# Fused attention, soft mixture of experts and feed-forward: the drain of attention reordered, w1 read by contiguous rows, three more places for weights, w_in narrowed in the experts, passage reordered

## The chip, the cores and the metric

The kernel runs on one core of one Trainium2 chip. The metric is the device time of one execution in microseconds (us), as the median over runs. Five engines work side by side and wait for each other by semaphores: TensorE (PE; its weight loads are shown apart as PEld), VectorE (DVE), ScalarE (ACT), GpSimd (POOL) and SyncE (SP). SP issues nearly all DMA transfers here, in one queue, in program order.

## The reference

```python
# attention: q, k, v are (4, 8, 576, 64); factor = 4
out_d     = sm_attn(mean4(q), mean4(k), mean4(v))      # on means of 4 tokens
out_up    = np.repeat(out_d, 4, axis=2)
out_local = softmax(where(|i - j| < 4, q k^T / 8, -1e9)) @ v
x = (out_up + out_local) as (2304, 512)
# soft mixture: phi (512, 32), w1 (8, 512, 1024), w2 (8, 1024, 512)
logits     = x @ phi
slot_input = softmax(logits, over tokens).T @ x        # 32 slots, 4 an expert
slot_out_e = relu(slot_input_e @ w1[e]) @ w2[e]
x = softmax(logits, over slots) @ slot_out
# feed-forward: w_in (512, 2048), w_out (2048, 512), both float64
h = relu(x @ w_in);  out = h * h @ w_out
```

## The kernel before, in words

**Attention** (to about 153 us) takes 16 units of two heads, in a software pipeline whose steps are single letters with a lag each; a table gives the order of the letters for each of 19 rounds. Each unit's output `xt` gives its share of the logits (`lgt`), and is transposed into token rows (`xk`, and `xr` for the last 64 tokens). Batch by batch, the softmax over tokens runs on with a running maximum `mb` and a factor `al` that rescales what has been summed: `acc = acc * al + new` (line 695) is the input of the 32 slots before normalisation, in four groups of rows.

**The drain** (lines 797 to 833) finishes the last batch. The exponentials `ee` are transposed and copied (`et`, `etr`); `mb` is transposed and its maximum over the four groups is taken (`mrow`); from it come the weights `wt` and the sum `ws`, and by `scales` the selection matrix `selw`, which joins the four groups and normalises. Four matmuls (`stp`) with the weights `acc` and the moving `selw` give `sT`, the transposed slot inputs. `busy(n)` issues n padding matmuls whose result nobody reads; `CHAIN` says how many stand at three places of the drain, and `FN` how many in each attention round.

**The experts** (lines 878 to 961): for each of eight, `expert_up` multiplies `sT` with the four pieces of w1 (`hp`, 32 matmuls), ScalarE applies relu (`hs`), a transpose (`htp`, copied to `ht`) and `expert_down` with four pieces of w2 (`so`, 32 matmuls) follow. Beside them run the softmax over slots (`gate_soft`, `gate_rows`) and, after two w2 pieces of expert 6, copies of the gates (`crp` into `cst`). `NEXP` says after which w2 piece of which expert a step of narrowing is recorded.

**Narrowing**: w_in and w_out come as float64 (pairs of 32-bit words) and become float32 by five operations on each 128 x 512 piece; the first, an absolute value, is on VectorE up to the end of the experts and on ScalarE after (`act_abs`). `NORDER` is the order of the pieces; `narrow_turn` goes one operation further with the pieces in hand, and begins the next turn's pieces ahead. `split_wout` (ScalarE) and `split_low` (VectorE) then split a w_out piece in a high part and a rest.

**The passage** (table `ACHAIN`): `S` copies `so` to `sos`, `T` transposes it to `soT` (`sotp`), `a` multiplies it with w_in (`ap`, copied to `asb`), `r` spreads it into rows (`arp`, copied to `ast`), `g` copies gates, `n` steps the narrowing, `W` splits a w_out piece, `f` issues padding matmuls, and `u` makes the first products `up` of the final stage.

**The final stage** (lines 1135 to 1160) runs 96 steps, 6 chunks of 384 tokens by 16 pieces of 128 hidden columns: one matmul `up`, relu (`r`), squares, high part `ghi` and rest `glo`, and nine matmuls `po`.

**Loads.** The weights are cut into loads of 128 x 4096 bytes. The list `loads` is w1 and w2 expert by expert, w_in 0 put in after the 43rd load (`LPOS`), then `TAIL`. `load_next` issues from the list's head as long as a place is free: 32 places of a ring, a few of other pools, among them two opened late in attention (`NLA`) and six opened when the tiles of the last unit are done (`NLB`). A place is free again when its piece's last matmul or narrowing is recorded, and the transfer then waits in the queue for that instruction. Each load also waits for the eighth load before it to land.

Of the kernel before, what the change touches and what calls it, by code (L numbers as in the profile page):

```python
# [20 lines left out]
NU = B * NP  # L21
DM = 512
# [27 lines left out]
FN = {'F': [0, 1, 1, 0, 0, 0, 0, 0, 0, 0, 0, 0, 0, 0, 0, 4, 0, 10, 0, 0], 'H': [10, 5, 2, 0, 0, 0, 0, 0, 0, 0, 0, 0, 0, 0, 0, 1, 0, 4, 6, 0], 'J': [1, 4, 3, 0, 0, 0, 0, 0, 0, 0, 0, 0, 0, 0, 0, 0, 7, 3, 0, 0]}  # L50
# [6 lines left out]
CHAIN = (5, 4, 4)  # L57
# [3 lines left out]

LPOS = [43, 43, 43, 43]
TAIL = 'o0 o1 i1 o2 o3 o4 o5 o6 o7 i2 o8 o9 o10 o11 i3 o12 o13 o14 o15'
SLOTS = {16: ['i1'], 20: ['r1'], 40: ['i2'], 44: ['r2'], 60: ['i3'], 70: ['r3']}
NORDER = 'w,w w,w o0 o1 o2 o3 w,w o4 w,w o5 o6 o7 o8 w o9 w,w o10 w o11 o12 w,w o13,w w o14 o15'
NEXP = {(5, 0): 1, (5, 1): 1, (5, 2): 1, (5, 3): 1, (6, 0): 1, (6, 1): 1, (6, 2): 1, (6, 3): 1}
WRES = 0
ACHAIN = 'S1 T n1 f1 g4 g2 g3 a0 f2 n4 f1 r0 r1 W0 f2 n2 n1 f2 u0 f3 n1 u1 f3'
# [5 lines left out]
NLA, NLB = 2, 6  # L74
# [5 lines left out]
def attention_moe_ffn_kernel(  # L80
# [23 lines left out]
    def bt(shape, name):  # L104
        return bank("t", shape, 3, name)
# [61 lines left out]
    def load(kind, i, j, place):  # L167
        pool, tag = where[kind, i, j] = place
        name = f"{kind}{i}_{j}"
        if kind in ("win", "wout"):  # L170

            t = pool.tile([128, 512, 2], I32, tag=tag, name=name)
            if kind == "win":
                src = w_in.bitcast(I32).rearrange("(t p) f -> p t f", t=4)[:, i, 1024 * j:1024 * j + 1024]
            else:
                src = w_out.bitcast(I32)[128 * i:128 * i + 128]
            nc.sync.dma_start(out=t.rearrange("p f w -> p (f w)"), in_=src)
        elif kind == "w1":
            t = pool.tile([128, FE], F32, tag=tag, name=name)
            nc.sync.dma_start(out=t, in_=w1[i].rearrange("(p t) f -> p t f", t=4)[:, j])  # L180
        else:
            t = pool.tile([128, 2, DM], F32, tag=tag, name=name)
            nc.sync.dma_start(out=t, in_=w2[i].rearrange("(j p t) f -> p j t f", j=4, t=2)[:, j])
        got[kind, i, j] = t
# [88 lines left out]
    def narrow_turn():  # L273
        if not current:
            new = not ahead
            narrow_ahead()
            if not ahead:
                return False
            current.extend(ahead)
            ahead.clear()  # L280
            count[0] = 1
            if new and xq is None:
                return True
        count[0] += 1
        for y, z in current:
            next(z)
        if count[0] == 2 and xq is not None:
            narrow_ahead()
        if count[0] == 5:
            for y, z in current:  # L290
                next(z, None)
            current.clear()
            count[0] = 0
        return True
# [14 lines left out]
    with tc.tile_pool(name="att", bufs=1, side="right") as ap:  # L309
# [360 lines left out]
        def stage_g2(b):  # L670
            gs = G[b]
            ee = gs["ee"]
            t, tr = sdb[:, 0:128], sdb[0:64, 128:256]
            nc.tensor.transpose(t, ee[:, 0:128], ident)
            nc.tensor.transpose(tr, gs["eb"].rearrange("p j c -> p (j c)"), ident)

            et = ee[:, 0:128]
            etr = ap.tile([64, 128], F32, tag="etr", name=f"etr{b}")
            nc.scalar.copy(out=et, in_=t)
            nc.scalar.copy(out=etr, in_=tr)  # L680
            gs.update(et=et, etr=etr)

        def stage_g3(b, between=None):
# [66 lines left out]

        have = set()
# [27 lines left out]
        for s in range(NU + LASTS):  # L779
            for x in ORDERS.get(s, ORDER) + ("a" if s == LATE else ""):  # L780
# [18 lines left out]
        t = bt([1, 128], "mtp")  # L799
        nc.tensor.transpose(t, mrun, ident)  # L800
        mrow = ap.tile([1, 32], F32, name="mrow")
        nc.vector.tensor_reduce(out=mrow, in_=t.rearrange("p (j s) -> p s j", j=4), axis=AX.X, op=ALU.max)
# [13 lines left out]
        def scales():  # L816
# [4 lines left out]
            nc.vector.tensor_tensor(out=sr, in0=sr, in1=wt, op=ALU.mult)  # L821
            nc.vector.tensor_scalar(out=selw, in0=sel[:, 0], scalar1=sr, scalar2=None, op0=ALU.mult)
# [152 lines left out]
    def split_low(f):  # L977
        nc.vector.tensor_tensor(out=wlo[f], in0=w32.pop(f), in1=whi[f], op=ALU.subtract)
# [213 lines left out]
```

## Time and profile before

| | us |
|---|---|
| median of 3 runs | 442.98 (441.65 to 446.29) |
| the profiled execution | 440.98 |
| its span, first to last instruction | 439.3 |
| PE busy in the span | 410.1 (93%) |
| DVE busy | 299.8 (68%) |
| ACT busy | 270.2 (62%) |
| POOL busy | 114.5 (26%) |

The span is what the trace covers; the execution's own time holds about 1.7 us more around it. Matmuls are pipelined and their ends are modelled, so a busy PE is not PE at its peak. The granted clock is the share of TensorE's full 2.4 GHz that it was given in a stretch; 0.50 is its other level, 1.2 GHz. In a timeline row, the bracket says how long the engine had been idle before and which instruction ended that. A row xN that merges N instructions runs from the first's start to the last's end, with the waits between them.

### The profile page before, as it was taken

Reading aid. Unit: us, or ns where it says so; the run is one execution under the profiler, and the core shown is the slowest. Engines: PE = TensorE matmul, PEld = TensorE weight load, DVE = VectorE, ACT = ScalarE, POOL = GpSimd, SP = SyncE. Lnnn points to the kernel's source line nnn. Section 1 sums busy time; section 2 is a strip of 40 time slices with the busy share of each in tenths; the row PEclk is TensorE's granted clock in tenths of the full one; section 3 lists DMA queues with packets and bytes.
Section 4 is the critical chain, followed back from the end, with each engine's and each line's share of the span. In section 5 each row is a group of like instructions: output and inputs, shape, how many; then the busy total and the mean of one; then the engine's idle time right before and its main releaser. Section 6 shows DMA issues by size and latency. Waiting matters only on the chain.

```text
span 439.3 us, 11682 instructions
## 1 busy us (share of the span) xinstructions
PE 410.1 (93%) x4550; PEld 311.0 (71%) x4550; DVE 299.8 (68%) x712; ACT 270.2 (62%) x671; POOL 114.5 (26%) x225
## 2 busy tenths in 40 slices
PE   7798998999889889997899999999999999999996
PEld 5566666667657655553588788888888888888884
DVE  3675766666667421464999999797899956775464
ACT  4587778767866311242798689676966655545650
POOL 7576556556565200030000240002300040000000
PEclk9999999999999987999999999999999999999999
DMA  6999999999811744999994001020000000011123
GB/s 176 352 253 300 282 313 291 262 277 320 205 35 33 232 155 140 400 407 408 409 409 177 1 0 49 0 98 0 1 0 0 2 0 2 0 72 73 72 75 142
DMA packets 43249, 70.55 MB, mean 161 GB/s; under 512 B 24378, under 2 KB 24634, under 8 KB 43194
## 3 DMA queue, kind: packets, MB, share of 16 engines
q1 hardware_dynamic: 43050, 69.68, 49.1%
q8 instruction: 36, 0.59, 0.6%
q14 instruction: 19, 0.16, 0.1%
q10 hardware_dynamic: 144, 0.13, 0.1%
HBM read 65.07 MB, written 4.72 MB: 159 GB/s over the span
## 4 chain that ended last, share of the span: by engine, by line
PE 56%; DMA 7%; DVE 1%; ACT 1%; issue 1%; DVEq 0%; ACTq 0%; SPq 0%
PE po L1120 45%; DMA w<-in_moe_w_dram 5%; PE up L1039 4%; PE hp L883 3%; DMA wout<-in_moe_w_out_dram 2%; PE so L912 1%; PE lgt L362 1%; PE ap L997 1%; PE stp L831 0%; PE sip L693 0%; PE sip L687 0%; DVE xt L594 0%; DVE acc L695 0%; ACT w L228 0%; PE lgt L610 0%
## 5 line engine op out<-in xcount | busy, mean ns | idle before, releaser
L1120 PE MATMUL po<-wparts,ghi 128*128 128x512 f32 x576 | 148.7, 392 | 0.5 <-ACT ghi L1047 0.5
L1120 PEld LDWEIGHTS po<-wparts,ghi 128*128 128x128 f32 x576 | 106.9, 188 | 20.8 <-ACT ghi L1047 0.9
L1044 ACT ACTIVATE r<-up 128x384 f32<-128x384 f32 x96 | 47.1, 491 | 57.2 <-PE up L1039 50.9
L1120 PE MATMUL po<-wparts,glo 128*128 128x512 f32 x288 | 81.9, 391 | 0.0
L1052 DVE TENSOR_TENSOR glo<-r,ghi 128x384 fp32r<-128x384 f32 x94 | 52.0, 556 | 21.7 <-ACT ghi L1051 18.3
L1120 PEld LDWEIGHTS po<-wparts,glo 128*128 128x128 f32 x288 | 53.8, 188 | 13.3 <-DVE glo L1052 1.3
L1024 POOL COPY selq<-asb 32x128 f32<-32x128 f32 x48 | 19.6, 409 | 142.0 <-ACT asb L1005 139.4
L1048 DVE TENSOR_TENSOR r<-r 128x384 f32<-128x384 f32 x48 | 26.8, 558 | 17.4 <-ACT ghi L1047 17.4
L1039 PE MATMUL up<-cst,ast 128*128 128x384 f32 x96 | 33.3, 347 | 0.0
L506 POOL TENSOR_TENSOR pl<-elp,sm 64x350 f32<-64x350 f32 x32 | 24.7, 773 | 31.8 <-PE tr L410 23.8
L417 ACT COPY kz<-tr 64x320 f32<-64x320 f32 (+1 forms) x48 | 20.5, 428 | 14.7 <-PE tr L410 14.0
L421 ACT ACTIVATE qt<-tr 64x320 f32<-64x320 f32 x64 | 28.1, 439 | 1.3
L1047 ACT ACTIVATE ghi<-r 128x384 fp32r<-128x384 f32 x50 | 26.3, 525 | 1.6
L1050 ACT ACTIVATE r<-r 128x384 f32<-128x384 f32 x46 | 24.2, 526 | 1.5
L1051 ACT CAST ghi<-r 128x384 fp32r<-128x384 f32 x46 | 23.6, 514 | 1.5
L463 DVE TENSOR_REDUCE mx<-s 128x10 f32<-128x350 f32 x16 | 8.3, 516 | 23.5 <-PE s L452 23.5
L434 POOL TENSOR_TENSOR s<-kz 64x288 f32<-64x288 f32 x32 | 21.2, 663 | 5.6 <-DVE kz L417 3.5
L1104 DVE TENSOR_TENSOR part<-po,part 128x512 f32<-128x512 f32 x36 | 22.5, 679 | 0.0
L1039 PEld LDWEIGHTS up<-cst,ast 128*128 128x128 f32 x96 | 18.0, 188 | 4.5 <-issue 0.6
L469 ACT ACTIVATE elp<-elp 128x350 f32<-128x350 f32 x16 | 7.9, 496 | 20.8 <-DVE elp L464 20.8
L452 PE MATMUL s<-kz,qt 128*29 128x70 f32 x640 | 13.0, 225 | 7.0 <-ACT qt L421 7.0
L883 PE MATMUL hp<-w,sT 128*32 128x256 f32 x256 | 18.4, 433 | 1.2 <-issue 0.8
(209 smaller groups left out, 719.2 us busy)
## 6 DMA issues: line engine op xcount, KB each, us to landing
w<-in_moe_w_dram SPq DMA_DIRECT2D x64, 512.0 KB, 7.6
win<-in_moe_w_in_dram SPq DMA_DIRECT2D x16, 512.0 KB, 10.1
wout<-in_moe_w_out_dram SPq DMA_DIRECT2D x16, 512.0 KB, 10.2
vw<-in_v_dram SPq DMA_DIRECT2D x62, 80.0 KB, 6.7
q<-in_q_dram SPq DMA_DIRECT2D x16, 288.0 KB, 6.6
k<-in_k_dram SPq DMA_DIRECT2D x16, 288.0 KB, 6.3
out_dram<-o SPq DMA_DIRECT2D x17, 256.0 KB, 2.1
vw<-in_v_dram SPq DMA_DIRECT2D x2, 64.0 KB, 2.5
```

The lines of the kernel that those rows point to most:

```text
L421: nc.scalar.mul(out=o, in_=i_, mul=1.0 / 128.0)
L506: nc.gpsimd.tensor_tensor(out=pl[r, :, c0:c0 + W], in0=el[r], in1=sm[r, 0:NB].unsqueeze(2).to_broadcast([64, NB, W]), op=ALU.mult,)
L883: nc.tensor.matmul(t[32 * g:32 * g + 32], sT[:, kt], got["w1", e, kt][:, 256 * g:256 * g + 256], start=(kt == 0), stop=(kt == 3), tile_pos ...
L1039: nc.tensor.matmul(t, ast[:, 128 * f:128 * f + 128], cst[:, c * n:c * n + n], start=True, stop=True)
L1044: nc.scalar.activation(out=r, in_=t, func=AF.Relu)
L1047: nc.scalar.activation(out=ghi, in_=r, func=AF.Square)
L1048: nc.vector.tensor_tensor(out=g, in0=r, in1=r, op=ALU.mult)
L1050: nc.scalar.activation(out=g, in_=r, func=AF.Square)
L1051: nc.scalar.copy(out=ghi, in_=g)
L1052: nc.vector.tensor_tensor(out=glo, in0=g, in1=ghi, op=ALU.subtract)
L1104: nc.vector.tensor_tensor(out=part[c, i], in0=po[c][i], in1=part[c, i], op=ALU.add)
L1120: nc.tensor.matmul(po[c][i], a[:, 128 * i:128 * i + 128], w[f], start=(first and w is whi and a is ghi), stop=(last and a is glo), skip_gr ...
```

## The change

What it does, by parts:

- **Drain.** The transpose of the running maximum and its reduction are recorded right after the last unit's token rows (`last_max`, called from the main loop). Of the padding matmuls, those of round 18 (`FN['H']`, 6) go, and `CHAIN` begins with 2 in place of 5: nine fewer. The last `xr` and the last `etr` are copied on VectorE instead of ScalarE. The last update of `acc` is cut into two halves. `selw` is made by one operation with two factors instead of two operations. The copy of the last logits (`keep_logits`) is put behind `sT`.
- **w1 by contiguous rows.** A w1 piece j is rows 128j to 128j + 127 instead of every fourth row from j. To match, `stp` takes 128 adjacent columns of `acc` as weights instead of every fourth.
- **Three places.** A pool `late_c` with three places opens when attention's tiles are released; `load_next` is called with nine instead of six. It closes with `late_b` after expert 5.
- **Narrowing.** Two steps of w_in 0 are put into expert 4. `AHD` starts the next turn two rows later once ScalarE takes the absolute values, and during the experts a w_out turn is not begun ahead.
- **Order of loads.** `TAIL` puts w_out 2 and 3 ahead of w_in 1.
- **Passage.** `ACHAIN` has another order: `soT` earlier in the queues, two gate copies later, 7 padding matmuls instead of 12.
- `PLOW` is empty: `split_low` stays on VectorE.

```diff
-FN = {..., 'H': [10, 5, 2, 0, ..., 1, 0, 4, 6, 0], ...}
+FN = {..., 'H': [10, 5, 2, 0, ..., 1, 0, 4, 0, 0], ...}
-CHAIN = (5, 4, 4)
+CHAIN = (2, 4, 4)
+AHD = 4
+PLOW = ()
-TAIL = 'o0 o1 i1 o2 o3 o4 o5 o6 o7 i2 ...'
+TAIL = 'o0 o1 o2 o3 i1 o4 o5 o6 o7 i2 ...'
-NEXP = {(5, 0): 1, ...}
+NEXP = {(4, 0): 1, (4, 2): 1, (5, 0): 1, ...}
-ACHAIN = 'S1 T n1 f1 g4 g2 g3 a0 f2 n4 f1 r0 r1 W0 f2 n2 n1 f2 u0 f3 n1 u1 f3'
+ACHAIN = 'S1 n1 T f1 g2 a0 f1 n3 r0 r1 g3 W0 u0 g4 f2 n2 u1 n1 f3'
-NLA, NLB = 2, 6
+NLA, NLB, NLC = 2, 6, 3
...
-            nc.sync.dma_start(out=t, in_=w1[i].rearrange("(p t) f -> p t f", t=4)[:, j])
+            nc.sync.dma_start(out=t, in_=w1[i, 128 * j:128 * j + 128])
...
-        if count[0] == 2 and xq is not None:
+        if count[0] == (AHD if act_abs else 2) and xq is not None and (act_abs or turns and turns[0][0][0] != "o"):
             narrow_ahead()
...
-            nc.scalar.copy(out=gs["xr"][:, cs], in_=t)
+            (nc.scalar.copy if u < NU - 1 else nc.vector.tensor_copy)(out=gs["xr"][:, cs], in_=t)
...
-            nc.scalar.copy(out=etr, in_=tr)
+            (nc.scalar.copy if b < B - 1 else nc.vector.tensor_copy)(out=etr, in_=tr)
...
-                nc.vector.scalar_tensor_tensor(out=acc, in0=acc, scalar=gs["al"], in1=t, op0=ALU.mult, op1=ALU.add)
+                for c in (slice(0, DM),) if b < B - 1 else (slice(0, DM // 2), slice(DM // 2, DM)):
+                    nc.vector.scalar_tensor_tensor(out=acc[:, c], in0=acc[:, c], scalar=gs["al"], in1=t[:, c], op0=ALU.mult, op1=ALU.add)
...
+        def last_max():
+            t = bt([1, 128], "mtp")
+            nc.tensor.transpose(t, G[B - 1]["mb"], ident)
+            mrow = ap.tile([1, 32], F32, name="mrow")
+            nc.vector.tensor_reduce(out=mrow, in_=t.rearrange("p (j s) -> p s j", j=4), axis=AX.X, op=ALU.max)
+            return mrow
...
+                    if x == "X" and s - LAG[x] == NU - 1:
+                        mrow = last_max()
...
-            nc.vector.tensor_tensor(out=sr, in0=sr, in1=wt, op=ALU.mult)
-            nc.vector.tensor_scalar(out=selw, in0=sel[:, 0], scalar1=sr, scalar2=None, op0=ALU.mult)
+            nc.vector.tensor_scalar(out=selw, in0=sel[:, 0], scalar1=sr, scalar2=wt, op0=ALU.mult, op1=ALU.mult)
...
         stage_g3(B - 1, scales)
-        keep_logits(B - 1)
         busy(CHAIN[2])
...
-        accv = acc.rearrange("p (k t) -> p t k", t=4)
         for kt in range(4):
-            nc.tensor.matmul(t[:, kt], accv[:, kt], selw, start=True, stop=True)
+            nc.tensor.matmul(t[:, kt], acc[:, 128 * kt:128 * kt + 128], selw, start=True, stop=True)
...
         nc.vector.tensor_copy(sT, t)
+        keep_logits(B - 1)
...
-    load_next(NLB)
+    lc = lb_scope.enter_context(tc.tile_pool(name="late_c", bufs=1, reuse_waits="tile"))
+    free.extend((lc, f"b{NLB + i}") for i in range(NLC))
+    load_next(NLB + NLC)
...
```

VectorE's queue in the drain, from the maximum of the last logits to the first row of the gates, before:

```order
L802 TENSOR_REDUCE mrow<-mtp 1x32
L811 TENSOR_TENSOR wt<-mb_3144,mbp 128x1
L666 SCALAR_TENSOR_TENSOR srun<-srun,al_3146,sb_3145 128x1
L814 TENSOR_TENSOR ws<-wt,srun 128x2
L819 TENSOR_SCALAR sr<-ssp 128x1
L820 RECIPROCAL sr<-sr 128x1
L821 TENSOR_TENSOR sr<-sr,wt 128x1
L822 TENSOR_SCALAR selw<-sel,sr 128x32
L695 SCALAR_TENSOR_TENSOR acc<-acc,al_3146,sip_3200 128x512
L643 COPY lst<-lgt 128x16
L833 COPY sT<-stp 128x128
```

The same queue at the same place in the changed kernel:

```order
L758 TENSOR_REDUCE mrow<-mtp 1x32
L640 COPY xr_2727<-av_1_3059 64x128
L682 COPY etr_3170<-sdb 64x128
L819 TENSOR_TENSOR wt<-mb_3144,mbp 128x1
L668 SCALAR_TENSOR_TENSOR srun<-srun,al_3146,sb_3145 128x1
L822 TENSOR_TENSOR ws<-wt,srun 128x2
L827 TENSOR_SCALAR sr<-ssp 128x1
L828 RECIPROCAL sr<-sr 128x1
L829 TENSOR_SCALAR selw<-sel,sr,wt 128x32
L698 SCALAR_TENSOR_TENSOR acc<-acc,al_3146,sip_3191 128x256 x2
L838 COPY sT<-stp 128x128
L645 COPY lst<-lgt 128x16
```

Two copies have come in ahead of `wt`, one multiplication has gone, `acc` is in two halves, and `lst` has moved from before `sT` to behind it.

VectorE's queue in the passage, before (`win_1` is the second half of w_in 0 in float32, `win_0_3285` and `win_0_3287` its raw pieces, `w_0` w_out piece 0 in float32 and `wout_0_3631` the raw piece):

```order
L229 TENSOR_SCALAR win_1_3749<-win_1_3749 128x512 x2
L226 TENSOR_SCALAR w_0_3754<-wout_0_3631 128x512
L230 TENSOR_SCALAR win_1_3749<-win_1_3749 128x512 x2
L231 SCALAR_TENSOR_TENSOR win_1_3749<-win_0_3285,win_1_3749 128x512
L231 SCALAR_TENSOR_TENSOR win_1_3749<-win_0_3287,win_1_3749 128x512
L990 COPY soT<-sotp 128x128
L232 SCALAR_TENSOR_TENSOR win_1_3749<-win_0_3285,win_1_3749 128x512
L232 SCALAR_TENSOR_TENSOR win_1_3749<-win_0_3287,win_1_3749 128x512
L229 TENSOR_SCALAR w_0_3754<-w_0_3754 128x512
```

And in the changed kernel:

```order
L232 TENSOR_SCALAR win_1_3668<-win_1_3668 128x512 x2
L233 SCALAR_TENSOR_TENSOR win_1_3668<-win_0_3226,win_1_3668 128x512
L233 SCALAR_TENSOR_TENSOR win_1_3668<-win_0_3228,win_1_3668 128x512
L234 SCALAR_TENSOR_TENSOR win_1_3668<-win_0_3226,win_1_3668 128x512
L234 SCALAR_TENSOR_TENSOR win_1_3668<-win_0_3228,win_1_3668 128x512
L231 TENSOR_SCALAR w_0_3827<-w_0_3827 128x512
L995 COPY soT<-sotp 128x128
L232 TENSOR_SCALAR w_0_3827<-w_0_3827 128x512
```

The first operation on w_out piece 0 has left this queue (it is now ScalarE's), all of w_in 0 stands ahead of `soT`, and so does the second operation on w_out piece 0, which waits for ScalarE's.

ScalarE's queue in the passage of the changed kernel, from `sos` to the first `ghi`:

```order
L1070 COPY sos<-so 128x256
L230 ACTIVATE w_0_3827<-wout_0_3600 128x512
L869 CAST cst<-crp_3836 128x4x128
L1010 COPY asb_3857<-ap_3840 128x128
L230 ACTIVATE w_1_3863<-wout_0_3632 128x512
L1018 CAST ast<-arp_3866 128x128
L1018 CAST ast<-arp_3870 128x384
L869 CAST cst<-crp_3876 128x4x128
L978 CAST wparts_3880<-w_0_3827 128x512
L1049 ACTIVATE r_0_3886<-up_0_3884 128x384
L1052 ACTIVATE ghi_0_3888<-r_0_3886 128x384
```

Before, three `cst` copies stood between `sos` and `asb`, and the absolute value of w_out piece 2 stood ahead of this `r`.

## Rows read from the trace of the kernel before

**Rows 1.** The page, chain that ended last: shares of the span by line.
```profile
PE po L1120 45%; DMA w<-in_moe_w_dram 5%; PE up L1039 4%; PE hp L883 3%; DMA wout<-in_moe_w_out_dram 2%; PE so L912 1%; PE lgt L362 1%; PE ap L997 1%; PE stp L831 0%; PE sip L693 0%; PE sip L687 0%; DVE xt L594 0%; DVE acc L695 0%; ACT w L228 0%; PE lgt L610 0%
```
**Rows 2.** Busy us by stretch: length, PE, PEld, DVE, ACT, POOL; clock, DMA share, GB/s.
```profile
153.00:156.40 3.40, 3.31 (x29) 2.48 (x23) 0.84 (x4) 1.10 (x4) 0.00 (x0) 0.51 0.95 276
156.40:159.90 3.50, 3.35 (x31) 1.76 (x29) 1.12 (x6) 1.01 (x5) 0.00 (x0) 0.99 0.69 279
159.90:163.20 3.30, 2.38 (x12) 1.76 (x10) 1.25 (x5) 0.00 (x0) 0.56 (x2) 1.00 0.00 0
163.20:170.00 6.80, 6.42 (x59) 3.24 (x63) 0.29 (x1) 0.38 (x1) 0.00 (x0) 0.51 0.03 4
170.00:196.40 26.40, 25.39 (x522) 14.16 (x518) 11.33 (x43) 8.21 (x33) 3.78 (x12) 1.00 0.98 373
196.40:206.00 9.60, 7.00 (x94) 2.36 (x86) 3.66 (x8) 1.74 (x4) 0.00 (x0) 1.00 1.03 408
206.00:215.90 9.90, 8.28 (x68) 4.73 (x68) 8.94 (x19) 5.68 (x13) 0.00 (x0) 1.00 1.03 410
215.90:436.00 220.10, 219.13 (x1053) 180.29 (x1053) 177.40 (x333) 146.99 (x291) 19.61 (x48) 1.00 0.16 63
```
**Rows 3.** Chain of waits in order of time, the drain: start us, us, what.
```profile
154.76 2.19 PE lgt L362 x11
...
160.62 0.75 DVE acc L695
161.50 0.60 PE lgt L362 x4
162.10 1.82 PE stp L831 x8
...
164.29 6.58 PE hp L883 x64
```
**Rows 4.** Groups by line and form, 151 to 165 us: busy us, mean ns.
```profile
L630 ACT COPY xk<-xp 128x512 f32<-128x512 f32 x1 | 0.6, 577 | 0.0
...
L679 ACT COPY ee<-sdb 128x128 f32<-128x128 f32 x1 | 0.3, 266 | 2.0 <-PE sdb L675 2.0
```
**Rows 5.** Groups by line, PE, 173 to 195 us: hp at full clock.
```profile
L883 PE MATMUL hp<-w,sT 128*32 128x256 f32 x168 | 10.6, 380 | 0.8 <-issue 0.8
```
**Rows 6.** Weight loads of lines 831 and 629: ns min/median/max.
```profile
L831 PEld LDWEIGHTS stp<-selw,acc x8: 309/329/329, 161.8 to 163.4; 128*128 128x128 f32 x8
...
L629 PEld LDWEIGHTS xp<-ident,xt x64: 137/141/230, 24.6 to 153.8; 128*128 128x128 f32 x64
```
**Rows 7.** Timeline of SP's queue: start us, us, what was issued.
```profile
143.66 5.88 SPq L180 DMA_DIRECT2D w<-in_moe_w_dram  x4
...
153.25 17.54 SPq L177 DMA_DIRECT2D win<-in_moe_w_in_dram  x4
```
**Rows 8.** Who waited for whom, 176 to 222 us: total us, times, longest.
```profile
DVE w L226 <- DMA wout<-in_moe_w_out_dram: 6.6, 1, 6.6
...
PE so L912 <- DMA w<-in_moe_w_dram: 2.5, 5, 0.6
```
**Rows 9.** Timeline of ACT in the passage: start us, us, instruction, idle before.
```profile
206.04 0.37 ACT L1065 COPY sos<-so 128x256 f32<-128x256 f32 x1 [5.05 <-PE so L912]
...
212.87 0.62 ACT L973 CAST wparts<-w 128x512 fp32r<-128x512 f32 x1
214.22 0.69 ACT L228 ACTIVATE w<-wout 128x512 f32<-128x512 f32 x1 [0.73 <-DMA wout<-in_moe_w_out_dram]
...
215.31 0.52 ACT L1047 ACTIVATE ghi<-r 128x384 fp32r<-128x384 f32 x1
```
**Rows 10.** Timeline of DVE in the passage.
```profile
208.85 0.28 DVE L990 COPY soT<-sotp 128x128 f32<-128x128 f32 x1
...
214.54 0.42 DVE L230 TENSOR_SCALAR w<-w 128x512 int32<-128x512 int32 x1
```
**Rows 11.** Timeline of PE at the end of the experts.
```profile
205.28 0.64 PE L912 MATMUL so<-w,ht 128*32 128x256 f32 x8 [0.29 <-DMA w<-in_moe_w_dram]
```

More of the change, by code (lines that the diff above doesn't have):

```diff
@@ L49 @@
 ORDERS = {0: 'YAsFvSgKToGdpDlHqJRPcEVewnMNXtQbmL', 1: 'YSgREVFvqdJwnGKLsmDAPeToHlptQbMcNX', 2: 'YFcVSgRLEvqJwnKdsmPDAeToptQbHlGMNX', 3: 'YgSREVLFvqJwnKdsmDAeToHPGplctQbMNX', 15: 'YJSgREVFLvqwndKsmDAeToPHGpctQbMlNX', 16: 'YFSgREVLvqJdwnKlsmGDAeToPHpctQbMNX', 17: 'YJEFSgRVLvqwnPTKdsMDAmeoGHlctQbNXp', 18: 'YEVFLvqJSgDeRwnKdsmAToGHPlptQbcMNX'}
-FN = {'F': [0, 1, 1, 0, 0, 0, 0, 0, 0, 0, 0, 0, 0, 0, 0, 4, 0, 10, 0, 0], 'H': [10, 5, 2, 0, 0, 0, 0, 0, 0, 0, 0, 0, 0, 0, 0, 1, 0, 4, 6, 0], 'J': [1, 4, 3, 0, 0, 0, 0, 0, 0, 0, 0, 0, 0, 0, 0, 0, 7, 3, 0, 0]}
+FN = {'F': [0, 1, 1, 0, 0, 0, 0, 0, 0, 0, 0, 0, 0, 0, 0, 4, 0, 10, 0, 0], 'H': [10, 5, 2, 0, 0, 0, 0, 0, 0, 0, 0, 0, 0, 0, 0, 1, 0, 4, 0, 0], 'J': [1, 4, 3, 0, 0, 0, 0, 0, 0, 0, 0, 0, 0, 0, 0, 0, 7, 3, 0, 0]}
 LATE = 16
@@ L60 @@
 NRING = 32
+AHD = 4
+PLOW = ()
 LPOS = [43, 43, 43, 43]
-TAIL = 'o0 o1 i1 o2 o3 o4 o5 o6 o7 i2 o8 o9 o10 o11 i3 o12 o13 o14 o15'
+TAIL = 'o0 o1 o2 o3 i1 o4 o5 o6 o7 i2 o8 o9 o10 o11 i3 o12 o13 o14 o15'
 SLOTS = {16: ['i1'], 20: ['r1'], 40: ['i2'], 44: ['r2'], 60: ['i3'], 70: ['r3']}
 NORDER = 'w,w w,w o0 o1 o2 o3 w,w o4 w,w o5 o6 o7 o8 w o9 w,w o10 w o11 o12 w,w o13,w w o14 o15'
-NEXP = {(5, 0): 1, (5, 1): 1, (5, 2): 1, (5, 3): 1, (6, 0): 1, (6, 1): 1, (6, 2): 1, (6, 3): 1}
+NEXP = {(4, 0): 1, (4, 2): 1, (5, 0): 1, (5, 1): 1, (5, 2): 1, (5, 3): 1, (6, 0): 1, (6, 1): 1, (6, 2): 1, (6, 3): 1}
 WRES = 0
-ACHAIN = 'S1 T n1 f1 g4 g2 g3 a0 f2 n4 f1 r0 r1 W0 f2 n2 n1 f2 u0 f3 n1 u1 f3'
+ACHAIN = 'S1 n1 T f1 g2 a0 f1 n3 r0 r1 g3 W0 u0 g4 f2 n2 u1 n1 f3'
 NSTEPS = (2, 2, 2, 2, 2, 2, 2, 2, 2, 2, 0, 2, 1, 3, 0, 2, 2, 1, 3, 2, 0, 1, 3, 0, 0, 0, 0, 1, 1, 1, 2, 1, 4, 0, 0, 2, 2, 2, 1, 1, 0, 0, 2, 3, 0, 2, 3, 0, 0, 1, 2, 1, 2, 1, 0, 2, 2, 1, 0, 1, 0, 2, 1, 2, 3, 1, 2, 2, 0, 3, 2, 2, 1, 0, 1, 3, 3, 2, 1, 0)
@@ L798, in attention_moe_ffn_kernel @@
         busy(CHAIN[0])
[L799 to L802, printed above, removed]
         stage_g2(B - 1)
@@ L977, in split_low @@
     def split_low(f):
-        nc.vector.tensor_tensor(out=wlo[f], in0=w32.pop(f), in1=whi[f], op=ALU.subtract)
+        (nc.gpsimd if f in PLOW else nc.vector).tensor_tensor(out=wlo[f], in0=w32.pop(f), in1=whi[f], op=ALU.subtract)
     sos = xp.tile([128, 256], F32, tag="hs", bufs=2, name="sos")
```

## The prediction

> **What bounds the kernel now.** I read the chain of waits first. TensorE holds it: the final stage alone (po) has 45% of the span, and two DMA pieces are the only other large entries that are not matmuls [rows 1]. Then I cut the span into stages with the view of busy times by stretch [rows 2]. From 215.9 us to the end PE works 219.13 of 220.10 us at full clock: a wall whose length the change leaves alone, since its matmuls stay. What can move is the moment at which it begins. Before it lie the drain of attention (153 to 164.3), the first two experts' hp (to 171), the other experts, and the passage (206 to 215.9). In the drain and the first hp the granted clock is twice down at 0.51, its 1.2 GHz level, with full clock between [rows 2]. The DMA engines stand still from 159.9 to 170 (shares 0.00 and 0.03); between 196.4 and 206 they are full at 408 GB/s, which is 1.285 us for a load of 524,288 bytes.
>
> The queue view says why they stood still: seven loads went out from 143.66 on, an eighth at 153.25, and the ninth, w_in piece 1, waited inside that last row, which runs 17.54 us [rows 7], because the program gives it a place that expert 1's w1 frees.
>
> **The change, part by part.**
>
> *Drain, front half.* Of the 11 padding matmuls that stood with 2.19 us on the chain ahead of the transpose for the running maximum [rows 3], 9 go (1.8 us at 0.2 each), and that transpose now stands ahead of the rest. What comes up behind: ScalarE still copies xk (0.58) before ee (0.27) [rows 4], and etr, now on VectorE, is copied after ee and ahead of wt, on which ws and the end of the drain wait. Laying these end to end moves acc from 160.62 to about 159.4: **1.2 us**; ends 0.5 (xr and etr, 0.3 each by the ee row, wholly in series, and 0.7 of hand-overs) and 1.8 (all the padding).
>
> *Drain, rear half.* From the start of acc to the first hp matmul were 164.29 - 160.62 = 3.67 us: acc 0.75, padding 0.60 that waited for the small copy lst behind acc, eight weight loads and matmuls of stp 1.82, the copy sT and hand-overs for the rest [rows 3]. Now lst is behind sT, acc comes in halves of about 0.4, and the first half of stp runs beside acc's second. The weights of stp become contiguous: a load took 329 ns with a step of four elements, 141 for a contiguous 128x128 tile [rows 6]. New path: 0.8 for acc, four loads with their matmuls 0.7, sT with its hand-over 0.4, together 1.9 us. Gain **1.8**; ends 1.0 (loads as slow as before: 4 x 0.2 more) and 2.2. The page TensorE: Matmul & The Clock Gate of the Trainium skill (section LDWEIGHTS) gives a load's time by its columns alone; by it the new layout would bring nothing and this term would be its lower end. Rows 6 speak against it: same columns, 2.3 times the time.
>
> *Clock under the first hp.* Its 64 matmuls took 6.58 us at clock 0.51 [rows 2, 3]; later, at full clock, 168 took 10.6 us [rows 5], so 64 take 4.0. The clock fell after a stretch in which PE worked 2.38 of 3.30 us [rows 2], idle around acc. That idle time goes and hp moves into its place. I take full clock: **2.5 us**; ends 0 and 2.5.
>
> *Three places more.* Pieces 1 to 3 of w_in go out before hp instead of after it. The first waits for the last padding matmul ahead of stp (about 159.8), the second for the copy xk, the third for no engine; queued behind them on SP are loads whose turn comes with expert 1's hp anyway. They run while the DMA engines stood still: 3 x 1.285 = 3.9 us less in the full stretch, besides the 1.2 + 1.8 + 2.5 = 5.5 by which all starts earlier. Expert 7's last weights, which PE met at 205.28 [rows 11], would come near 195.9. Worth something there is only what PE waited: so waited 2.5 us for weights, all in the last two experts [rows 8]. I keep 0.3 for the short ScalarE copy ahead of the last one: **2.2**; ends 1.0 and 2.5. Late next is PE itself, the experts' matmuls in their order.
>
> *w1 by contiguous rows.* The stream that mixes both kinds of reads ran at 408 and 410 GB/s in its full stretches [rows 2], and PE waited for weights only at the end. **0**; cover is 3.9 us of lead, and a reading 10% slower or faster (1.3 us over ten loads) stays within it.
>
> *Passage.* Before, VectorE's queue held the first operation on w_out piece 0 ahead of the rest of w_in: it stood 6.6 us until that piece landed [rows 8], with four more w_in operations between it and the copy soT, which began at 208.85, 2.81 us after sos at 206.04 [rows 9, 10]. Now w_in 0 is narrowed within the experts; ahead of soT stand sos itself (0.37), one absolute value on ScalarE (0.69) and one VectorE operation (0.42) [rows 9, 10]: soT 1.6 us after sos. That is a wait the change adds: soT, and PE's ap behind it, now hang on w_out piece 0; it lands a load after expert 7's weights, near 197.2, before sos (198.3). At the other end ScalarE stood 0.73 us for w_out piece 2, with r and ghi of the first step queued behind [rows 9]; pieces 2 and 3 now go ahead of four w_in loads (5.1 us earlier), and that operation comes after ghi. Following ScalarE from the start of sos: the rest of the way to the end of asb shortens like soT, to 3.4; then an absolute value 0.7, the two ast copies behind arp until 5.2, cst and wparts 0.6 each (512 columns both), r and ghi 0.5 each (sizes by rows 9), and hand-overs: the first po 7.9 us after sos, against 215.9 - 206.04 = 9.9. Gain **2.0**; ends 0.7 (only the w_out wait) and 2.7.
>
> *The rest.* The merged multiplication for selw is in the drain's count. In the final stage the narrowing keeps its turns, and beginning a turn later (AHD) costs nothing while VectorE works 177 of 220 us there [rows 2]; if that cover were short, each late turn would hold PE for one operation, 0.7 us.
>
> **Sum:** 1.2 + 1.8 + 2.5 + 2.2 + 2.0 = 9.7 us. The execution goes from its own 440.98 (span 439.3) to 431.3. The median of the runs, 442.98, lies 2.0 above that execution; on that scale, on which I forecast, it is **433.3**.
>
> **Rivals.**
> A: the clock stays at half through the first hp, as before. For it: between 163.2 and 170 it did not come back although PE worked 6.42 of 6.80 us [rows 2]. Against it: the idle time ahead is gone. Without the 2.5 it is 435.8.
> B: the clock falls in the thinned passage or at the start of the final stage. Padding behind the last expert goes from 12 matmuls to 7, and PE worked 8.28 of 9.90 us there [rows 2]. Two stretches like that at 153 (3.4 us each) at half speed cost 3.4 us of matmul time: 436.7, and with A 439.2.
> C: the stream stays the bound, because the early loads slip behind hp or the queue loses their time elsewhere; the change does then not do what it says. The weights end 5.5 earlier, the passage keeps 1.5, since w_out piece 0 now holds soT: 7.0 in all, 436.0.
> D, slower: with nine padding matmuls less the clock stays at half from the drain through the experts. Their work takes 6.58/4.0 = 1.6 of its time then. The 7.2 us of the other terms are lost once 12 of the 26.4 us of experts [rows 2] run so; if all do, it costs 16, and the time is 452. For it: the 6.8 us at half with hp running; against it: full clock on the same work from 170 on [rows 2]. The rule behind it is on the page TensorE: Matmul & The Clock Gate of the Trainium skill (Part 1): the throttled state is the default, and activity releases it. The trace agrees in kind, 0.51 after idle stretches.
>
> **Chances.** Forecast 0.50, A 0.22, B 0.14, C 0.08, D 0.06. A measurement of this kernel can tell about 1%, 4.4 us. Below 438.55 lie the forecast, A, C and some 0.06 of B: faster 0.86. The rest of B is within 1%, 0.08. D is slower, 0.06. The range: all upper ends, 4.0 + 2.5 + 2.5 + 2.7 = 11.7, lead from 440.98 to 429.3; at the other side it takes in A, C and B at its worst. So 429.5 to 439.5.
>
> **What would show it.** Afterwards: acc near 159.4 and hp near 161.3; hp's 64 matmuls in about 4 us at clock 1.00; DMA engines busy between 160 and 164; no so waiting for weights in the last two experts; soT within 2 us of sos; the first po near 206, and 220 us from there to the end. I am wrong if po comes earlier but the last stage grows beyond 221 us, if hp is on time and still takes 6.6 us (A), or if weights still end the waits of the last experts (C).

## The result, and the profile after

The changed kernel takes **431.3 us** (median of 4 runs, 430.58 to 431.98) against 442.72 for the kernel before (441.65 to 446.29): a ratio of 0.9728, 95% interval 0.9671 to 0.9785, 11.4 us. The forecast was 433.3, in the range 429.5 to 439.5. The profiled execution took 431.98 us with a span of 430.3; before it was 440.98 and 439.3, 9.0 us more. Medians are over all executions; ratios, their intervals (95%, in square brackets) and mean clocks leave out slow ones, those more than 1.5% above the fastest of the same kernel.

The page of the changed kernel, its chain that ended last, shares of the span by line (as [rows 1]):

```profile
PE po L1125 44%; PE up L1044 4%; PE so L917 4%; PE hp L888 3%; PE ap L1002 1%; DVE glo L1057 0%; DVE part L1107 0%; PE lgt L364 0%; DVE r L1053 0%; PE warm L930 0%; PE ctp L722 0%; DVE win L234 0%; DVE win L233 0%; PE arp L1015 0%; PE crp L867 0%
```

The two DMA pieces that held 7% of the span are gone in this profile: the chain now stays on TensorE nearly all the way. Busy times by stretch, columns as in [rows 2]; the last three rows run from the end of the first hp to sos, from there to the first po, and to the end of the last po:

```profile
153.00:156.40 3.40, 2.96 (x34) 2.19 (x34) 1.61 (x8) 0.95 (x3) 0.00 (x0) 0.60 1.03 282
156.40:159.90 3.50, 3.50 (x26) 1.46 (x25) 1.46 (x8) 0.65 (x3) 0.04 (x1) 0.90 0.81 324
159.90:163.20 3.30, 2.89 (x40) 1.97 (x41) 1.13 (x4) 0.27 (x1) 0.52 (x2) 1.00 0.48 118
163.20:170.00 6.80, 6.59 (x143) 3.83 (x135) 1.51 (x6) 1.41 (x6) 0.12 (x1) 1.00 1.02 402
...
165.49:196.66 31.17, 30.44 (x584) 16.36 (x576) 18.20 (x56) 9.96 (x38) 5.12 (x12) 1.00 1.03 408
196.66:204.96 8.30, 6.41 (x61) 4.48 (x61) 5.83 (x13) 6.49 (x15) 0.00 (x0) 1.00 1.03 410
204.96:424.60 219.64, 218.91 (x1054) 180.29 (x1053) 176.78 (x330) 147.08 (x290) 20.27 (x48) 1.00 0.17 64
```

In 163.2 to 170 us TensorE gets through 143 matmuls at clock 1.00, where before it did 59 at 0.51 in the same time; the DMA engines are full there (402 GB/s) instead of idle. The chain of waits from the drain to the first hp (start us, us, what), and the weight loads of stp:

```profile
159.75 0.54 PE lgt L364 x4
160.29 0.03 issue
160.32 1.09 PE stp L836 x8
161.41 0.02 issue
161.43 0.30 DVE sT L838
161.74 0.04 issue
161.78 3.71 PE hp L888 x64
```

```profile
L836 PEld LDWEIGHTS stp<-selw,acc x8: 186/192/192, 160.3 to 161.1; 128*128 128x128 f32 x8
```

stp takes 1.09 us for 1.82 and its loads 192 ns for 329; hp takes 3.71 for 6.58 [rows 3, 6]. Who waited for whom in the experts and the passage, TensorE's rows, 160 to 222 us (total us, times, longest):

```profile
PE up L1044 <- ACT cst L874: 1.1, 1, 1.1
PE sotp L994 <- ACT sos L1070: 0.5, 1, 0.5
PE so L917 <- issue: 0.4, 1, 0.4
PE hp L888 <- DVE sT L838: 0.4, 1, 0.4
...
```

No so (the experts' second product) waits for a weight any more (2.5 us in [rows 8]). The longest wait left in the passage is a new one: up for a gate copy. VectorE's queue there shows soT behind the operation on w_out piece 0:

```profile
197.62 0.43 DVE L231 TENSOR_SCALAR w<-w 128x512 f32<-128x512 f32 x1 [2.29 <-ACT w L230]
197.97 0.28 DVE L995 COPY soT<-sotp 128x128 f32<-128x128 f32 x1
```

sos begins at 196.66, soT 1.31 us later instead of 2.81. One execution is a thin base here, so both kernels were profiled once more. This table reads the same marks from each trace (chain and timelines):

| stage, us | before | again | changed | again | mean gain | forecast |
|---|---|---|---|---|---|---|
| last logits to acc | 7.77 | 6.89 | 6.34 | 6.50 | 0.9 | 1.2 |
| acc to first hp | 3.67 | 3.68 | 2.00 | 2.00 | 1.7 | 1.8 |
| hp, 64 matmuls | 6.58 | 6.43 | 3.71 | 3.71 | 2.8 | 2.5 |
| end of hp to sos | 35.17 | 34.87 | 31.17 | 31.36 | 3.8 | 2.2 |
| sos to first po | 9.85 | 9.84 | 8.30 | 8.55 | 1.4 | 2.0 |
| first po to last | 219.2 | 219.2 | 219.6 | 219.6 | -0.4 | 0 |
| last po to end | 4.23 | 4.14 | 5.71 | 5.55 | -1.4 | 0 |

With attention, whose end comes 0.5 us later, the rows make the 8.15 us between the mean spans (438.35 and 430.2). The medians above lie some 3 us further apart: both profiled executions of before are among its quick ones, and in the comparisons it ran anywhere between 436.75 and 447.25 us. Over all executions on record with their clock, 60 of before and 8 of the changed kernel, the medians are 441.1 and 431.7, 9.5 us apart, so the 11.4 of the first four and four is a large draw. Their mean granted clock is 0.989 before and 0.996 changed; one stretch of 3.4 us at half clock takes 0.004 from such a mean. So an execution of the changed kernel has about two such stretches fewer on average, more than the profiles show (0.988 and 0.992 before, 0.992 twice after).

In the second profile of the changed kernel a DMA piece is on the chain again, ahead of soT:

```profile
186.69 10.15 DMA wout<-in_moe_w_out_dram
```

This is w_out piece 0, landing at 196.84 when sos had begun at 196.37; soT came 1.60 us after sos there.

### The profile page after: what moved, and what is told of

The parts are those of the page before. It is cut to its first block, busy times and chain, and to the rows that moved or that the text cites. A ratio compares the mean times of both kernels' runs of the same rounds, so it can differ in the third digit from the quotient of the medians.

```text
span 430.3 us, 11647 instructions
## 1 busy us (share of the span) xinstructions
PE 402.4 (94%) x4534; PEld 308.2 (72%) x4534; DVE 300.7 (70%) x713; ACT 270.6 (63%) x670; POOL 116.2 (27%) x225
## 4 chain that ended last, share of the span: by engine, by line
PE 59%; DVE 3%; ACT 1%; issue 1%; DVEq 0%; ACTq 0%
PE po L1125 44%; PE up L1044 4%; PE so L917 4%; PE hp L888 3%; PE ap L1002 1%; DVE glo L1057 0%; DVE part L1107 0%; PE lgt L364 0%; DVE r L1053 0%; PE warm L930 0%; PE ctp L722 0%; DVE win L234 0%; DVE win L233 0%; PE arp L1015 0%; PE crp L867 0%
## 5 line engine op out<-in xcount | busy, mean ns | idle before, releaser
L517 POOL TENSOR_TENSOR pn<-pd,sm 128x435 f32<-128x435 f32 x16 | 14.6, 914 | 15.5 <-DVE sm L516 7.9
## 6 DMA issues: line engine op xcount, KB each, us to landing
win<-in_moe_w_in_dram SPq DMA_DIRECT2D x16, 512.0 KB, 10.2
wout<-in_moe_w_out_dram SPq DMA_DIRECT2D x16, 512.0 KB, 10.2
```

## The experiments

**1. The three places undone.**

```diff
-NLA, NLB, NLC = 2, 6, 3
+NLA, NLB, NLC = 2, 6, 0
```

> The changed kernel without its three further places for weights (NLC 0); all else as changed. Theory P, the forecast's term: in the changed kernel the last expert weights land near 195.2 us and TensorE reaches them at 195.4 to 195.9, a lead of some 0.5 us; without the places three loads of 1.285 us fall back behind expert 1's hp, so the DMA engines stand still again from about 160 to 164 us and the weights of the last two experts come 3.9 us later. so waits 2 to 3.4 us for weights there, sos starts near 199.5 and the time is 433.5 to 434.7. Rival Q: the 5.4 us by which the drain and hp now end earlier feed the stream enough, and the experts' 4.0 us came from something else than the waits for weights: so waits under 0.5 us for weights, time 431.3 to 431.8.

Measured: 435.21 us (10 runs), ratio to before 0.9886 [0.9846, 0.9925]. Busy times by stretch, and two rows of the view of who waited:

```profile
163.20:167.50 4.30, 3.92 (x83) 2.42 (x82) 0.37 (x2) 0.38 (x1) 0.00 (x0) 1.00 0.05 14
167.50:203.14 35.64, 32.84 (x584) 16.95 (x576) 18.10 (x56) 9.95 (x37) 4.82 (x12) 0.95 1.01 396
```

```profile
PEld so L917 <- DMA w<-in_moe_w_dram: 4.9, 6, 1.1
PE so L917 <- DMA w<-in_moe_w_dram: 2.5, 4, 0.6
```

The DMA engines stand again under hp (share 0.05), the experts take 35.64 us as before, and so waits 2.5 us for weights again. Part of the 35.64 is the clock: TensorE was at half clock at the end of this stretch.

```profile
199.50:203.14 3.64, 3.06 (x18) 0.54 (x18) 0.00 (x0) 0.00 (x0) 0.00 (x0) 0.54 1.03 405
```

So the profile alone does not size the term; TensorE's busy time is 32.84 us there against 31.6 in before. By the medians the places are worth 3.1 to 3.9 us. Theory P holds in what it says of the DMA engines and the waits; the time is 0.5 us above its range. An earlier drain does not feed the stream, because the stream starts with the end of hp and moves with it.

**2. No padding while acc is made.**

```diff
-CHAIN = (2, 4, 4)
+CHAIN = (2, 4, 0)
```

> The changed kernel without the 4 padding matmuls that run while VectorE makes acc (CHAIN 2, 4, 0); TensorE stands about 0.6 us there. Theory A (the clock under the first hp hangs on that idle time): the granted clock in the stretch of the first hp falls to about 0.5, its 64 matmuls take about 6.6 us instead of 3.7, and the time is 433 to 434.5. Theory F (what freed the clock is the rest: hp moved close behind the drain, no wait for lst): hp stays at 3.7 us and clock 1.00, time 431.0 to 431.8.

Measured: 431.34 us, ratio 0.9787 [0.9676, 0.9898]. The stretches around acc and under hp:

```profile
159.50:161.60 2.10, 1.14 (x12) 0.99 (x12) 1.24 (x4) 0.00 (x0) 0.56 (x2) 1.00 1.06 402
161.60:165.30 3.70, 3.70 (x81) 2.31 (x81) 0.01 (x1) 0.38 (x1) 0.00 (x0) 1.00 0.71 260
```

TensorE works 1.14 of 2.10 us and the clock stays at 1.00 all the way. Standing around acc did not bring the clock down in this execution: theory A's reason fails there, and the time is F's.

**3. The old layout of the hidden features.**

```diff
-nc.sync.dma_start(out=t, in_=w1[i, 128 * j:128 * j + 128])
+nc.sync.dma_start(out=t, in_=w1[i].rearrange("(p t) f -> p t f", t=4)[:, j])
...
-    nc.tensor.matmul(t[:, kt], acc[:, 128 * kt:128 * kt + 128], selw, ...)
+    nc.tensor.matmul(t[:, kt], accv[:, kt], selw, ...)
```

> The changed kernel with the old layout of the hidden features: w1 read by interleaved rows (every fourth row) and the weights of stp taken from acc with a step of four elements. Theory L, the forecast's: the eight weight loads of stp go from 192 to about 329 ns each, stp from 1.08 to about 1.8 to 2.1 us, hp starts 0.7 to 1.1 later, and the reading of w1 costs nothing (DMA engines full at 406 to 410 GB/s as with contiguous rows): time 431.9 to 432.6. Rival by columns alone (a load's time does not know the step): loads stay at 192 ns, time 431.3 to 431.6. Rival D2: interleaved rows make the stream slower, under 395 GB/s in 170 to 190 us, and so waits for weights in the last experts: time above 433.

Measured: 436.16 us (10 runs), ratio 0.9918 [0.9877, 0.9959]: much more than theory L gave. The loads of stp are back at 329 ns and stp at 2.04 us (+0.95), as L said:

```profile
L837 PEld LDWEIGHTS stp<-selw,acc x8: 308/329/329, 161.6 to 163.2; 128*128 128x128 f32 x8
```

hp took 5.38 us, because a stretch at half clock fell on it:

```profile
164.00:167.50 3.50, 3.43 (x34) 1.59 (x38) 0.10 (x2) 0.00 (x0) 0.00 (x0) 0.51 0.87 344
```

That is 2.6 of the 4 to 5 us. The stream ran at 387 GB/s in 170 to 190 us (408 in the changed kernel), below the 395 that D2 named, and the time is above D2's 433; but only one weight load waited, 0.4 us, so D2's late weights did not come. Whether the rest is the reading of w1 through attention, runs 7, 11 and 12 ask.

**4. The old order of passage and loads.** ACHAIN and TAIL are as before; the narrowing of w_in 0 in the experts stays.

```diff
-TAIL = 'o0 o1 o2 o3 i1 ...
+TAIL = 'o0 o1 i1 o2 o3 ...
-ACHAIN = 'S1 n1 T f1 g2 a0 f1 n3 r0 r1 g3 W0 u0 g4 f2 n2 u1 n1 f3'
+ACHAIN = 'S1 T n1 f1 g4 g2 g3 a0 f2 n4 f1 r0 r1 W0 f2 n2 n1 f2 u0 f3 n1 u1 f3'
```

> The changed kernel with the old order of the passage (ACHAIN) and the old order of loads behind the experts (TAIL); the earlier narrowing of w_in in the experts stays. Theory of the forecast: soT comes early all the same, since w_in 0 is narrowed in the experts, but ScalarE stands again for w_out piece 2 ahead of r and ghi (0.7 us before): from sos to the first po 9.0 to 9.9 us instead of 8.5, time 431.8 to 432.8. Rival: the order is worth nothing, since in the changed order TensorE stands 1.14 us for the gate copy of the tail tokens (cst) that the old order makes before ap: 8.5 us or less from sos to the first po, time 430.5 to 431.5.

Measured: 432.21 us, ratio 0.9821 [0.9741, 0.9902]. From sos to the first po 8.58 us (198.22 to 206.80): the 0.7 us for w_out piece 2 are back, the wait for the tail cst is gone, and the one pays for the other: neither side's range for this way (9.0 and more, 8.5 and less) was met. By elimination, what the passage gained is nearly all the earlier narrowing; no run undid the narrowing alone. The new order adds 0.0 to 0.3 us here, and 0.7 in the last stage, which took 220.3 us in run 4 for 219.6. The drain, which is that of the changed kernel word for word, met a stretch at half clock under hp here (5.39 us). Against these stands an end behind the last matmul that is 1.3 us shorter (4.3 us; last section). The median lies in the range of the forecast's theory, but hardly apart from the changed kernel's 431.3 and 432.13.

**5 and 6. Both kernels once more.**

> The changed kernel once more, for a second profile and for times beside the other kernels of this row. Theory C (the stretches at half clock come once or twice between 150 and 170 us and fall elsewhere in each execution): hp's 64 matmuls may take anything from 3.7 to 6.6 us, the time stays 430 to 433. Theory F (the change freed the clock under the first hp for good): hp takes 3.7 us again, clock 1.00 from 161 to 168 us.

> The kernel before once more, for a second profile. Theory F: the clock is at about 0.5 under the first hp again, which takes some 6.6 us, since TensorE stands idle around acc in every execution. Theory C: the stretch at half clock lies elsewhere or is missing, hp takes 4.0 to 5.5 us; time 437 to 446 by the spread so far.

Measured: the changed kernel 432.13 us against 443.76, ratio 0.9797 [0.9700, 0.9895]; the single time of before 439.18. hp took 3.71 and 6.43 us: theory F for these two, C for run 4.

**7. w1 by interleaved rows, stp contiguous.** Only the first line of run 3's diff.

> The changed kernel with w1 read by interleaved rows as before, while stp keeps its contiguous weights; the rows of w1 then no longer stand in the order of the features, so the experts multiply other rows than the reference does, the amount of work being the same. Theory W (of the 4.9 us that the old layout cost together, most is the reading: w1 pieces are read through attention, where q, k and v wait in the same queue): 433.5 to 436, share of the queue in 20 to 125 us 97 to 98% against 92 to 96%. Theory of the forecast (the reading costs nothing): 431 to 432, and the 4.9 us were stp's weight loads (1.0), the clock (1.7) and chance.

Measured: 433.77 us, ratio 0.9818 [0.9694, 0.9942], beside 432.13 for the changed kernel on the same chip. 1.6 us with intervals that overlap: the median lies in theory W's range, but the four runs don't settle it. The queue had a share of 103% in 20 to 125 us, above W's 97 to 98, and hp took 3.70 us.

**8. The old drain, with stp contiguous, places and passage as changed.**

```diff
-CHAIN = (2, 4, 4)
+CHAIN = (5, 4, 4)
...
-                    if x == "X" and s - LAG[x] == NU - 1:
-                        mrow = last_max()
...
         busy(CHAIN[0])
+        mrow = last_max()
```

FN, the two copies, acc in one piece, the place of keep_logits and the two operations for selw go back likewise.

> The changed kernel with the old drain: the padding of 5 and 11 matmuls ahead of the transpose of the maximum, both copies on ScalarE, acc in one piece, the last logits copied behind acc, two operations for selw; stp's contiguous weights, the three places and the new passage stay. Theory F (drain and clock as forecast): hp starts 1.7 to 2.3 us later and takes 6.6 us at half clock: 435.5 to 437. Theory C (the clock under hp is not the drain's doing): only the later start is left, less what the DMA stream hides: 432.5 to 434. Rival: the loads' lead takes it all, 431.3 to 432.

Measured: 434.02 us, ratio 0.9858 [0.9761, 0.9954], 1.9 us above the changed kernel on the same chip. The chain there:

```profile
160.58 0.75 DVE acc L698
161.33 0.10 DVE lst L645
161.43 0.04 issue
161.47 0.60 PE lgt L364 x4
162.07 0.83 PE stp L837 x8
162.89 0.02 issue
162.92 0.30 DVE sT L839
163.22 0.04 issue
163.26 5.29 PE hp L888 x64
```

acc to hp is 2.68 us: of the 1.7 that the rear half of the drain gained, 1.0 is stp's layout and 0.7 the order. hp took 5.29 us, between the 3.7 of full clock and the 6.6 that theory F gave. The time is at the upper end of theory C's range: the contiguous weights alone did not hold the clock in this execution.

**9 and 10. Three gate copies earlier; and ten padding matmuls more.** In 9, crp 2 takes the place of the padding in expert 7, the tail crp runs while TensorE waits for sos, and crp 3 ahead of ap.

```diff
-ACHAIN = 'S1 n1 T f1 g2 a0 f1 n3 r0 r1 g3 W0 u0 g4 f2 n2 u1 n1 f3'
+ACHAIN = 'S1 n1 g4 T f1 g3 a0 f1 n3 r0 W0 r1 u0 f2 n2 u1 n1 f3'
-BETWEEN = {..., (7, 2): (7,)}
+BETWEEN = {..., (7, 2): (2,)}
```

In 10, besides, FN's H gets 10 for 4 at step 17, and a new entry puts 4 ahead of values_down.

> The changed kernel with three copies of the gate moved in the passage: crp 2 takes the place of the two padding matmuls in expert 7, the tail tokens' crp goes behind the last so into TensorE's wait for sos, crp 3 ahead of ap, and wparts of w_out piece 0 between the two ast copies. Theory S (the passage is ScalarE's series from asb to the first ghi, and the 1.14 us that TensorE stood for the tail cst): the first po comes 2.0 to 2.4 us earlier after sos, 6.2 to 6.6 us instead of 8.3, and the time is 429 to 430 where the changed kernel has 431.3 to 432.1. Rival K (the second w_out piece is late then: wparts 1 is ready no earlier, and TensorE stands at the third step instead): what is gained before the first po is lost within the first 10 us of the final stage, 431 to 432. Rival E (crp 2 in expert 7 delays so, since no slack is left there): sos 0.4 to 0.7 later, 430 to 431.

> The same with ten more padding matmuls in the two waits of the last attention step: 4 ahead of av's down part (TensorE stood 0.59 us there) and 6 more ahead of the last logits (0.88 us). Theory C1 (the clock falls in the drain because TensorE stands in 149.6 to 153 us): clock 1.00 from 150 to 170, the way from the last logits to acc 5.7 us as in the run without a fall, instead of 6.3 to 6.5, and the time 0.5 to 1 us less than without this padding. Rival C2: the fall comes all the same, at another place between 150 and 170, and the time is the same within 0.5; if it comes under hp, 1.5 to 2.9 more.

Measured: 431.47 us, ratio 0.9767 [0.9719, 0.9815], and 430.40 us, ratio 0.9755 [0.9709, 0.9801]. The passage did nearly what S said (6.2 to 6.6): 6.66 us from sos to the first po. What it gained went where K said, and the time is K's. Run 9, who waited on TensorE from 204 us to the end:

```profile
PE po L1125 <- DVE glo L1057: 0.8, 1, 0.8
PE po L1125 <- DVE wparts L983: 0.5, 1, 0.5
PE po L1125 <- ACT part L1107: 0.3, 1, 0.3
```

The third step's po stands for w_out piece 1, and the last stage takes 221.05 us for 219.6. The clock was 1.00 from 145 to 175 us in run 10, and half from 160.2 to 163.6 in run 9. Theory C1 fits that one execution, but run 2 showed the same without the added padding. Run 10 has the lowest median of all, a difference of 0.9 us to the changed kernel that these intervals do not separate.

**11 and 12. In the kernel before, the layout alone; the reading of w1 alone.** The lines of run 3 the other way round, and of these the first only.

> The kernel before with only the layout changed: w1 by contiguous rows and stp's weights contiguous. Theory W (reading w1 contiguously relieves the queue through attention): 437 to 440 where the kernel before has 441 to 444, share of the queue in 20 to 125 us 92 to 96% against 97.5 and 99.8%. Theory of the forecast (the reading is worth nothing, the layout only stp's loads): hp starts 0.8 to 1.0 earlier, and since the last experts wait for the stream, which starts with hp's end, 0.5 to 1.0 us less: 440.5 to 443.

> The kernel before with w1 read by contiguous rows and nothing else; stp keeps its strided weights, so the experts multiply other rows than the reference does, the amount of work being the same. Together with stp's contiguous weights this reading gave 438.56 against 441.62 us (ratio 0.9929). Theory W (most of that is the reading): ratio 0.993 to 0.997, 1.3 to 3 us faster. Theory of the forecast (the reading is worth nothing, stp's loads 1.0 us and the clock under hp the rest): ratio 0.998 to 1.002.

Measured: 438.56 us, ratio 0.9929 [0.9889, 0.9968] for the layout; 440.31 us, ratio 0.998 [0.9947, 1.0012] for the reading alone (12 runs each). The first is a miss: 438.56 lies in the range of theory W and below the 440.5 to 443 of the forecast's theory. But the reading alone gained nothing that can be measured, 0.9 us at the middle of its interval, so by the middles most of the layout's 3.1 us comes with stp's contiguous weights; the two intervals overlap. The queue did get relief from the reading, as W had it: its share in 20 to 125 us was 97.5 to 103.0% in the four profiles with interleaved rows and 91.4 to 97.6% in the ten with contiguous ones. It was not worth time. The chain of the layout alone:

```profile
161.97 0.30 DVE sT L832
162.28 0.04 issue
162.32 3.71 PE hp L882 x64
```

The old drain, old padding and old passage, and hp still runs at full clock. All the profiles, by the way stp takes its weights:

| stp's weights, drain | time of hp, us (one profile each) |
|---|---|
| step of four, old drain | 6.58 (before), 6.43 (again), 5.13 (run 12) |
| step of four, new drain | 5.38 (run 3) |
| contiguous, old drain | 3.71 (run 11), 5.29 (run 8) |
| contiguous, new drain | 3.71 (changed), 3.71 (again), 3.71 (1), 3.71 (2), 5.39 (4), 3.70 (7), 5.37 (9), 3.71 (10) |

## Why the prediction was right, point by point

**The wall.** It stood: 219.6 us from the first po to the end of the last, 219.2 before. All that was gained was gained ahead of it, as the forecast had it. The forecast's 9.7 us lies between the 8.15 of the pairs of profiles and the 11.4 of the first medians.

**Drain, front half** (1.2): 0.9 in the mean of the pairs. Where no stretch at half clock falls into it, the way from the last logits to acc is 6.89 us old (before again, run 8) and 5.66 new (run 2): 1.23.

**Drain, rear half** (1.8): 1.7. Weight loads of the same columns took 192 ns for 329. They did not come down to the 141 of rows 6: the step costs a factor of 1.7 here, not 2.3. The page TensorE: Matmul & The Clock Gate of the Trainium skill (section LDWEIGHTS) gives a load's time by its columns alone; these rows do not agree with it.

**Clock under the first hp** (2.5): 2.8 in the pairs, but for a reason that the forecast did not give. It credited the idle time around acc. Run 2 has that idle time and full clock. Run 8 has the old idle time and a half-slowed hp, run 11 the old idle time and full clock. So the step that credited the clock to that idle time failed. With stp's weights at a step of four, hp met half clock in 4 profiles of 4; with contiguous ones in 3 of 10. If the layout had no part in it, so uneven a split would come up about once in 29 times (120 of 3432 ways). The mean clocks of whole executions lean the same way: 0.992 over the 10 of run 3 against 0.995 over 39 with contiguous weights and the new drain, and 0.993 in run 11 against 0.989 for before on its chip, while the reading of w1 alone (run 12) gave 0.990 against 0.989. They also lean towards the drain, 0.992 in the four executions of run 8. So the layout probably carries part of this term, the order of the drain may carry some, and why the clock does so stays open. Rival A (0.22) came true in neither profile of the changed kernel, and by some 1.7 us in runs 4 and 9, which have the same drain.

**Three places** (2.2, ends 1.0 and 2.5): this is the term that was mis-sized. It measured 3.1 to 3.9 us in run 1, and 3.8 in the pairs of profiles. The prediction said that the places are worth only what PE waited, and took the waits that TensorE's rows name, 2.5 us in [rows 8]. Beside them TensorE stood 0.79 us within one hp of the first profile of before, put down to nothing, and its busy time itself shrank, 31.6 to 30.5 us for the same 584 matmuls: by the profile's account a row broken by a wait pays the end of its last matmul each time, 0.64 us for 8 against 1.93 for 32 in one piece (ends of matmuls are modelled). Late next was TensorE, as said, though by little: the last piece of expert 7's w2 was issued at 185.0 us and lands 10.2 later, near 195.2, and TensorE has other work until 195.4.

**w1 by contiguous rows** (0): held, at -0.9 us with an interval from -2.3 to 0.5 (run 12). The reading behind it did not: the stretches at 408 and 410 GB/s in [rows 2] hold no w1 load, since the last went out by 185.0 us and landed before 196. From 180.87 to 190.87 us, with w1 pieces under way, before moved 409 GB/s, so the conclusion stands.

**Passage** (2.0, first po 7.9 us after sos): 1.4, at 8.30 and 8.55. soT came 1.31 and 1.60 us after sos (forecast 1.6); in the second profile it hung on w_out piece 0, the wait that the prediction said the change adds, since that piece landed 0.47 us after the start of sos and not 1.1 before it. The series of ScalarE was even quicker than summed: the first ghi was done at 203.53, 6.87 us after sos. What failed is the last step, that the first po follows ghi. TensorE's queue holds the second up ahead of it, and that waits for the gate copy of the tail tokens, which stands behind ghi on ScalarE; three padding matmuls and the third up follow before po:

```profile
203.44 0.35 ACT L874 CAST cst<-crp 128x256 fp32r<-128x256 f32 x1
```

```profile
203.84 0.44 PE L1044 MATMUL up<-cst,ast 128*128 128x384 f32 x1 [1.14 <-ACT cst L874]
```

```profile
204.28 0.66 PE warm L930 x3
```

The change added this wait when it moved that copy from ahead of asb to behind the first ghi; the forecast followed one engine's queue and not the other's.

**The rest** (0): 0.4 us went in the last stage, where TensorE stood 0.5 us for a glo and 0.2 us for a sum of earlier po (`part`), and 1.4 behind the last matmul (below). Neither was in the sum. Together they ate what the places gave beyond 2.2.

**Rivals.** B: the clock stayed at 1.00 in the passage and up to the last matmul, though the padding went from 14 matmuls to 7 and not from 12. C: no wait for weights is left in the experts; it is what run 1 looks like. D: full clock on all experts. So the forecast's case came. That its sum came so near is luck: two errors, +1.6 in the places and -1.8 at the end, met.

## What to carry to other kernels

When weights arrive by a stream that a freed place starts, everything ahead of that place moves the stream as well, so here only places that were free earlier gave it lead. The waits that the profile named, 2.5 us, were less than what ending them gained, 3.1 to 3.9 us, since broken rows of matmuls took longer too. Follow every queue at a hand-over, not just the one that seems to carry the chain: here an up stood ahead of po. One profile of an execution is one draw: the stretches at half clock moved from run to run, and a second profile of both kernels was worth more than a further argument.

## What the runs showed of the hardware

**The clock falls at another place in each execution.** In a view by half microseconds, 3 of the 14 profiles have no stretch at a granted clock of 0.50 (1.2 GHz) between 145 and 175 us (runs 2, 10 and 11), 10 have one, and the first of before has two. Most such stretches are 3.3 to 3.5 us long, those under hp in the two profiles of before 6.8, and they begin anywhere between 153 and 164 us. TensorE worked 2.57 of 3.00 and 3.21 of 3.60 us ahead of the fall in run 4, and 1.14 of 2.10 without one behind it in run 2, so these rows don't tell when it comes.

**The last output write lands late in the new order.** Behind the last matmul the changed kernel took 5.7 us for 4.2. Time from issue to landing of the 19 output writes, min, median and max, in before and in the changed kernel:

```profile
DMA to landing us min/median/max: 2.0/2.1/2.6
```

```profile
DMA to landing us min/median/max: 2.0/2.2/3.9
```

What the DMA engines moved in the last 7 us of the changed kernel, in 40 slices:

```profile
GB/s 0 0 0 0 0 0 0 0 82 339 363 339 363 410 339 363 357 328 334 363 322 100 23 23 23 23 23 23 0 0 0 0 0 0 0 0 0 0 0 0
```

23 GB/s, about a sixteenth of the 322 to 410 ahead of it, goes on for over a microsecond: by the rate, one of the 16 engines is still at it when the others are done. The end took 5.1 to 5.7 us in every profile with the new order of loads, and 4.1 to 4.3 in every one with the old order of loads and passage (both of before, runs 4, 11 and 12). Why one engine is behind was not tried and stays open.
